# An attention and two MoE layers on one core: buffers at multiples of 256 bytes, three small operations rewritten, the planner's constants replaced

## The chip, the cores and the metric

One core of one Trainium2 chip runs the whole program in one launch. The metric is the device time of an execution in microseconds, and of several executions the median. The engines are named as in the profile: PE is TensorE's matmul and PEld its weight load, DVE is VectorE, ACT is ScalarE, POOL is GpSimd, SP is SyncE, whose queue issues all DMAs of this kernel.

## What is computed

An attention with a decay (4 batches, 8 heads, 576 positions, 64 dimensions), then two pairs of dense layers that are called MoE (2304 tokens, 512 wide, 2048 inside), the second with a slope per column. All is float32.

```
scores = scale * q @ k.T + (cum[:, None] - cum[None, :])      # cum: running sum of log f
scores = where(causal, -1e9, scores); scores -= max(scores)
attn = exp(scores); attn = attn / (sum(attn) + 1e-9)
x = attn @ v                                                   # to (2304, 512)
h = x @ w_in;   x = max(0.01 * h, h) @ w_out                   # first MoE
h = x @ w_in2;  out = (max(h, 0) + alpha * min(h, 0)) @ w_out2 # second MoE
```

## The kernel before

Products are made at float32's accuracy from `float32r` operands: a tile is split into a high part (a cast) and a low part (the tile minus its high part), and PE adds three products, high times high, high times low and low times high. Nearly all work of ACT, DVE and POOL is there to make such pairs.

**Stages.** The attention works in eight groups, four of 320 query rows and four of 256 (`ORDER`, `GROUPS`), in units of up to 128 rows (`UNITS`). The first 16 heads (`NAT`) are "native": they skip the splits and use PE's slower float32 matmul, in the prologue, while the first weights arrive. The others are spread over the first MoE, as work between its matmuls. The first MoE runs over blocks of 256 or 512 tokens (`BLOCKS`): for each of 16 chunks f of the inner width, `moe_h` (L604) makes h, `leaky` (L613) the activation, `hi` and `lo` its split, `moe1_y` (L650) the product with w_out. Of its 32 half chunks of weights 14 stay in SBUF and 18 (`STREAM`) are written to `wscr` and read back for each block through the ring `ws`. The second MoE takes three blocks of 768 tokens with a Strassen-like scheme of seven products (`moe2_h`, L761; `moe2_y`, L830); its combined weights are made earlier by `weight2_in` and stored in `w2in`. Raw weights come as 64-bit floats, and `assemble` puts float32 numbers together from their halves on ACT (L492, the "rebase") and DVE (L499, L502, L507).

**One attention unit** (`attention_scores`, `attention_weights`): PE makes scores (L1131), POOL masks the decay row `cb` into `dm` by a selection (L1097) or, for packed pairs of heads, adds a mask (L1104), DVE adds it to the scores and takes the row's extreme into `nm` (L1145, the "decay"), ACT takes the exponential and the row sum (L1156), DVE adds 1e-9 to the sum (L1001, the "guard") and inverts it (L1004), for two units at once, and ACT, POOL or DVE multiply by the inverse (L1171, L1173, the normalisation). PE then transposes (L1186), ACT and DVE split the transposed tile into `pt` (L404, L1202), and PE multiplies by v (L1034). `shift` (L1075, ACT) and `add` (L1078, DVE) bring the two parts of v's product together, and the result is split into `xp`.

For a head that isn't native, `qk` holds q and k twice, in the upper and the lower 64 partitions. `qk_hi` casts both into `k1`, `q_lo` (L935) overwrites the lower 64 partitions of q's columns with q's low part, by DVE or POOL, and `k_lo` makes k's low part in `k2`. v lies in DRAM with a block of 64 zeros between the two heads of a pair, which the native heads need; `vr` loads it with the zeros (L914), and `v_hi` and `v_lo` split it into `v2`.

**The order of the work.** Every operation is handed to a planner (`Plan`) with its engines, its assumed duration on each, a due time and the buffers that it reads and writes. `Plan.run` goes through time, gives each engine the ready operation with the earliest due time, and the program is written in that order; on the chip every engine works strictly in its order and waits on semaphores. `latency` (L121) is what the planner allows between the end of an operation on one engine and the start of one that needs it on another: 260 ns to PE, 200 from PE, 170 otherwise, 125 on the same engine, `DMALAT` after a DMA. The due times come from the constants at the top of the file: `PROL`, `PROL0` and `FIRST0` are the assumed lengths of the prologue and the first block, `LEAD1`, `LEAD2` and `LASTSPAN` say how early a group of the attention is due, `AHEAD` how early a streamed weight, the constants of `W2` when the second MoE's weights are made, `PACKLEAD` how early the first scores of a pair.

**Where the tiles lie.** Tiles are placed one after another in pools, each rounded up to 32 bytes. The 8 bytes of `rate` and the 4 of `warm` put `xp` and all that follows in the pool `sb` (the rings `g`, `gr`, `w`, `ws`, `ysb`, `tri`) at 192 bytes past a multiple of 256. In the pool of the attention the 80 bytes of `nm` move what follows by 96. In the pool `p2` of the second MoE the 64 bytes of `alpha` bring what follows to a multiple of 256: `bx`, `yraw`, `xt`, `r`, `g2`, `wb` and the last of the four `wa`. What is placed from the right (`raw`, `cv`, later `by`) lies 224 past one.

Of the kernel before, what the change touches and what calls it, by code (L numbers as in the profile page):

```python
# [26 lines left out]
AHEAD = 7600  # L27
# [4 lines left out]
PACKLEAD = 5200  # L32
# [14 lines left out]
W2LEAD = 112200  # L47
NEARLY = 4
W2FROM = 2.77
W2EACH = 0.68  # L50
W2LAG = 51000
W2STEP = 5300
W2OUT = 8400
# [7 lines left out]
PROL = 52000  # L61
PROL0 = 26000
FIRST0 = 99000
FREE = 8
ATTN = 12800
LASTH = 10600
W1LEAD = 12500
LEAD1 = 24000
LEAD2 = 54900
DMALAT = 2600  # L70
BATCH = 1
LASTSPAN = 1.04
STEP = 4
PRICE = 0.25
# [36 lines left out]
class Plan:  # L111
# [165 lines left out]
def t_act(n):  # L277
    return 0.833 * n + 90
# [14 lines left out]
def t_pool1(n):  # L293
    return 0.833 * n + 245
# [19 lines left out]
def tile_forgetting_attention_two_moe(ctx: ExitStack, tc, qk0, qk1, v0, v1, fg, w1, w2, alphaT, out):  # L314
# [78 lines left out]
    dram = ctx.enter_context(tc.tile_pool(name="dram", bufs=1, space=DRAM))  # L393
    vctx = ExitStack()
# [49 lines left out]
    ring("vr", 2, [P, 5, 3, D], pool="att")  # L444
# [6 lines left out]
    ring("nm", 3, [P, 4, 5], pool="att")  # L451
# [6 lines left out]
    ring("nm0", 4, [P, 4, 5], pool="att0")  # L458
# [3 lines left out]
    rate = const.tile([B * H, 2], F32, name="rate")  # L462
    warm = const.tile([1, 1], F32, name="warm")
# [5 lines left out]
    warm_b, cum_b, yd_b, wscr_b, w2_b, rate_b = (Buf(Ring(1, None)) for _ in range(6))  # L469
    for b, ap in ((warm_b, warm), (cum_b, cum_d), (yd_b, yd), (wscr_b, wscr), (w2_b, w2in), (rate_b, rate)):  # L470
        b.ap = ap
# [9 lines left out]
    def assemble(which, f, half, d, after=()):  # L481

        raw, v = new("raw"), new("cv")
        src = (w1, w2)[which].bitcast(I32)[f, :, 2 * CW * half : 2 * CW * (half + 1)]

        def load():
            sp.dma_start(out=raw.ap, in_=src.rearrange("p (n t) -> p n t", t=2))

        def rebase(e):
            high = f32(raw.ap[:, :, 1])  # L490
            if e == "act":
                act.activation(out=f32(v.ap), in_=high, func=AF.Copy, scale=2.0**-112)  # L492
# [19 lines left out]
        plan.op({"act": t_act(CW), "pool": t_pool1(CW)}, d, rebase, r=[raw], w=[v])  # L512
# [357 lines left out]
    def attention_heads(gi, hs, d, span):  # L870
# [29 lines left out]
        for e, h in enumerate(hs):  # L900
# [33 lines left out]
            def q_lo(en, k1=k1, qk=qk):  # L934
                sub(en, k1.ap[D:P, :n], qk.ap[D:P, :n], f32(k1.ap[D:P, :n]))  # L935
# [60 lines left out]
        for i, u, t, es, du in todo:  # L996
            if i % RECIPS == 0:
                i1 = min(i + RECIPS, len(todo))

                def guard(i=i, i1=i1):  # L1000
                    dve.tensor_scalar(out=nm.ap[:, 3, i:i1], in0=nm.ap[:, 2, i:i1], scalar1=1e-9, scalar2=None, op0=ALU.add)  # L1001
# [5 lines left out]
                on("dve", 70, du, guard, w=both)  # L1007
# [5 lines left out]
    def attention_out(g, t0, h, e, dd, vr, v2, o2, lo, hi, pt, pt_ap, native):  # L1013
# [68 lines left out]
        on("act", t_act(n) - 40, dd, shift, r=[po], w=[(xr, h % 2)])  # L1082
        on("dve", t_dve(n), dd, add, r=[po], w=[(xr, h % 2)])
# [170 lines left out]
    for i in range(2):  # L1254
        rows = sum(max(0, min(NAT - gi * H, H)) for gi, k in enumerate(ORDER) if k == i)
# [75 lines left out]
    ring("alpha", 1, [P, NF], pool="p2", after=opened)  # L1331
# [86 lines left out]
```

## Time and profile before

| | us |
|---|---|
| median of 3 runs | 993.36 |
| lowest and highest | 992.1 and 994.47 |
| the profiled execution, its own time | 991.83 |
| its span, first to last instruction | 989.7 |
| PE busy | 976.0 |
| DVE busy | 746.7 |
| ACT busy | 536.2 |
| POOL busy | 90.1 |

The busy times say how long an engine had at least one instruction in work. A matmul's end is modelled, and matmuls overlap in the picture, so PE's pace is read from how many of them a stretch holds. The first MoE and the attention last until about 608 us; the second MoE takes the rest.

### The profile page before, as it was taken

How to read it: one execution, taken by the hardware profiler on the slowest of the kernel's cores; microseconds unless marked ns; L12 is line 12 of the kernel's file. 1: busy time of each engine (PE TensorE's matmuls, PEld its weight loads, DVE VectorE, ACT ScalarE, POOL GpSimd, SP SyncE). 2: the span in 40 equal slices, each digit the busy share in tenths (PEclk: the TensorE clock that was granted, in tenths of full speed). 3: DMA queues.
4: the chain of work that ended last, by engine and by line, in shares of the span. 5: the costliest groups of instructions: out<-in, count | busy, mean ns of one | idle time of the engine just before them, and what ended most of it. 6: DMA issues, size and time to landing. Idle time of an engine off the chain costs nothing.

```text
span 989.7 us, 15662 instructions
## 1 busy us (share of the span) xinstructions
PE 976.0 (99%) x5170; PEld 842.6 (85%) x5170; DVE 746.7 (75%) x1849; ACT 536.2 (54%) x1231; POOL 90.1 (9%) x161
## 2 busy tenths in 40 slices
PE   9999999999999999999999999999999999999998
PEld 7777777999888878878878888889889898988987
DVE  7798999887998897986776647856696656856563
ACT  8987887996887777867646435211232112321112
POOL 2101233211211120211000000000000000000000
PEclk9999999999999999999999999999999999999999
DMA  8869887688767789845497765533374333634311
GB/s 285 286 202 320 284 316 229 207 297 285 259 228 267 242 275 320 271 145 174 138 368 253 262 213 173 175 111 118 107 245 129 127 118 107 203 121 144 105 46 64
DMA packets 76128, 203.27 MB, mean 205 GB/s; under 512 B 8112, under 2 KB 23248, under 8 KB 76048
## 3 DMA queue, kind: packets, MB, share of 16 engines
q1 hardware_dynamic: 76048, 202.28, 61.2%
q8 instruction: 41, 0.67, 0.3%
q14 instruction: 39, 0.32, 0.1%
HBM read 168.57 MB, written 33.67 MB: 204 GB/s over the span
## 4 chain that ended last, share of the span: by engine, by line
PE 76%; DVE 10%; issue 6%; DMA 4%; ACT 4%; POOL 1%; POOLq 0%; ACTq 0%; SPq 0%; DVEq 0%
PE bank L830 20%; PE bank L761 18%; PE bank L650 12%; PE bank L604 12%; PE bank L1131 5%; PE bank L1186 3%; PE bank L1034 3%; DMA raw<-w 2%; PE bank L1024 1%; DVE pt L1202 1%; DVE k L409 1%; DVE t L1145 1%; DMA w2in<-wa 1%; DVE cv L507 1%; DVE g L409 1%
## 5 line engine op out<-in xcount | busy, mean ns | idle before, releaser
L830 PE MATMUL bank<-w,g 128*128 128x512 f32 x756 | 196.9, 393 | 0.0
L404 ACT ACTIVATE g<-r 128x384 fp32r<-128x384 f32 x96 | 50.4, 526 | 256.3 <-DVE r L793 232.5
L770 DVE TENSOR_TENSOR r<-bank,r 128x384 f32<-128x384 f32 x168 | 91.0, 555 | 91.1 <-PE bank L761 90.9
L830 PEld LDWEIGHTS bank<-w,g 128*128 128x128 f32 x756 | 140.1, 188 | 21.2
L650 PE MATMUL bank<-g,ws 128*128 128x512 f32 (+1 forms) x540 | 128.0, 374 | 1.3 <-ACT g L404 1.3
L604 PE MATMUL bank<-xp,ws 128*128 128x512 f32 (+1 forms) x540 | 126.3, 372 | 0.0
L650 PEld LDWEIGHTS bank<-g,ws 128*128 128x128 f32 x540 | 92.1, 189 | 18.2 <-ACT g L404 3.7
L604 PEld LDWEIGHTS bank<-xp,ws 128*128 128x128 f32 x540 | 93.3, 189 | 15.2
L650 PE MATMUL bank<-g,w 128*128 128x512 f32 (+1 forms) x420 | 101.4, 375 | 0.1
L604 PE MATMUL bank<-xp,w 128*128 128x512 f32 (+1 forms) x420 | 99.2, 374 | 0.1
L1156 ACT ACTIVATE t<-t,nm 128x128 f32<-128x128 f32 (+4 forms) x144 | 83.9, 586 | 24.6 <-DVE nm L1145 24.2
L604 PEld LDWEIGHTS bank<-xp,w 128*128 128x128 f32 x420 | 72.1, 189 | 12.4 <-ACT t L1171 0.5
L650 PEld LDWEIGHTS bank<-g,w 128*128 128x128 f32 x420 | 71.8, 189 | 12.1 <-ACT g L404 0.7
L1202 DVE TENSOR_TENSOR pt<-bank,pt 128x128 fp32r<-128x128 f32 (+2 forms) x136 | 64.1, 504 | 22.2 <-ACT pt L404 21.7
L1097 POOL TENSOR_SCALAR_AFFINE_SELECT dm<-cb 128x448 f32<-128x448 f32 (+1 forms) x96 | 54.9, 573 | 264.1 <-DVE nm L1145 224.2
L1171 ACT ACTIVATE t<-t,nm 128x128 f32<-128x128 f32 (+4 forms) x112 | 58.8, 564 | 28.7 <-DVE nm L1004 27.5
L409 DVE TENSOR_TENSOR g<-r,g 128x384 fp32r<-128x384 f32 x96 | 53.2, 554 | 25.9 <-ACT g L404 25.9
L404 ACT ACTIVATE pt<-bank 128x512 fp32r<-128x512 f32 (+6 forms) x176 | 67.6, 433 | 4.3 <-PE bank L1186 3.6
L1186 PE MATMUL bank<-tri,t 128*128 128x128 f32 x432 | 65.8, 277 | 1.7 <-DVE t L1173 0.5
L409 DVE TENSOR_TENSOR g<-gr,g 128x512 fp32r<-128x512 f32 x72 | 50.4, 700 | 18.4 <-ACT g L404 18.3
L1186 PEld LDWEIGHTS bank<-tri,t 128*128 128x128 f32 x432 | 49.3, 141 | 15.0 <-ACT t L1171 5.3
L1034 PEld LDWEIGHTS bank<-pt,v 128*128 128x128 f32 x416 | 55.8, 189 | 5.9 <-ACT pt L404 1.9
(136 smaller groups left out, 1687.0 us busy)
## 6 DMA issues: line engine op xcount, KB each, us to landing
ws<-wscr SPq DMA_DIRECT2D x72, 512.0 KB, 4.9
raw<-w SPq DMA_DIRECT2D x64, 512.0 KB, 5.8
wa<-w2in SPq DMA_DIRECT2D x33, 512.0 KB, 3.5
ws<-w2in SPq DMA_DIRECT2D x33, 512.0 KB, 3.5
qk<-qk SPq DMA_DIRECT2D x32, 416.0 KB, 4.7
wscr<-ws SPq DMA_DIRECT2D x18, 512.0 KB, 5.6
cb<-cum_d SPq DMA_DIRECT2D x32, 288.0 KB, 4.4
vr<-v SPq DMA_DIRECT2D x16, 480.0 KB, 5.1
```

What stands on the lines that cost most here:

```text
L404: act.activation(out=out, in_=in_, func=AF.Copy)
L409: (dve if e == "dve" else gps).tensor_tensor(out=out, in0=in0, in1=in1, op=ALU.subtract)
L604: pe.matmul(h()[:, i] if single else h(), lhsT=w.ap[:, a, c * P : (c + 1) * P], rhs=xs[0].ap[:, s, c] if single else xp[:, x0 : x0 + 2, s, c],
L650: pe.matmul(out(c), lhsT=w.ap[:, a, col : col + P], rhs=g.ap[:, s, at : at + n], start=f == 0 and (a, s) == (0, 0) and (c % 2 == 0 or not ...
L761: pe.matmul(b.ap[:, :N2], lhsT=t.ap[:, a, o + c * P : o + (c + 1) * P], rhs=view(k)[:, s, c], start=c == 0 and i == 0, stop=c == 1 and i == 2,
L770: on("dve", t_dve(N2), d + k * step - URGENT, lambda: dve.tensor_tensor(out=out.ap, in0=b.ap[:, :N2], in1=x.ap, op=ALU.add), r=[b] if x is ...
L830: pe.matmul(acc[j * (N2 // P) + t].ap, lhsT=g.ap[:, s, t * P : (t + 1) * P], rhs=w.ap[:, a], start=p == 0 and i == j and (a, s) == (0, 0), ...
L1034: pe.matmul(po.ap[:, q:n], lhsT=v2.ap[:, o2 + j, :], rhs=pt_ap(s, e, j, j + 1, q, n), start=s == 0 and j == 0, stop=s == 1 and j == nkt - 1,)
L1156: act.activation(out=t.ap[:, :nk], in_=t.ap[:, :nk], func=AF.Exp, scale=-1.0, bias=nm.ap[:, last, u : u + 1], accum_out=nm.ap[:, 2, u : u ...
L1171: act.activation(out=t.ap[:, :nk], in_=t.ap[:, :nk], func=AF.Copy, scale=nm.ap[:, 3, u : u + 1])
L1186: pe.transpose(tp.ap[:, (j - j0) * P : (j - j0 + 1) * P], t.ap[:, k0 : k0 + P], f32(tri_b.ap[:, :P]))
L1202: dve.tensor_tensor(out=lo, in0=src, in1=f32(hi), op=ALU.subtract)
```

## The change

1. **Addresses.** `rate` and `warm` move into one tile `small` of 128 bytes, together with `alpha` and a new column `lower`; a tile `edge` of 224 bytes is placed first from the right; `nm` has rows of 16 instead of 5 numbers (256 bytes instead of 80). With that every tile from `xp` on starts at a multiple of 256 bytes.
2. **q's low part.** `lower` is 0 in the upper 64 partitions and -1 in the lower. `q_lo` becomes one operation over all 128 partitions, lower * k1 + qk, which leaves q's high part above and its low part below; it runs on DVE alone.
3. **The guard** runs on POOL instead of DVE.
4. **v without zero blocks.** For heads that aren't native the load takes every second block of 64 columns; `vr` has two blocks per key tile instead of three.
5. **The planner.** Four of its latencies become constants with new values (125 on the same engine and 200 from PE as before, 315 to PE, 200 otherwise), the assumed times of the rebase, `shift` and `add` are 50, 130 and 100 ns longer, and 20 constants of the due times change.

```
-AHEAD = 7600
+AHEAD = 5100
-PACKLEAD = 5200
+PACKLEAD = 6100
...
-DMALAT = 2600
+DMALAT = 3200
...
+        return (0 if a == "pe" else TOSAME) if a == b else TOPE if b == "pe" else FROMPE if a == "pe" else CROSS
...
+    ctx.enter_context(tc.tile_pool(name="edge", bufs=1, side="right")).tile([P, 56], F32, name="edge")
...
-    ring("vr", 2, [P, 5, 3, D], pool="att")
+    ring("vr", 2, [P, 5, 2, D], pool="att")
...
-    ring("nm", 3, [P, 4, 5], pool="att")
+    ring("nm", 3, [P, 4, 16], pool="att")
...
-    rate = const.tile([B * H, 2], F32, name="rate")
-    warm = const.tile([1, 1], F32, name="warm")
+    small = const.tile([P, 32], F32, name="small")
+    rate, lower, warm = small[: B * H, :2], small[:, 2:3], small[:1, 3:4]
+    rings["alpha"] = Ring(1, lambda slot: small[:, 4 : 4 + NF])
...
-                    out=vr.ap[:, :nkt], in_=g["v"][b, h // 2]), w=[vr])
+                    out=vr.ap[:, :nkt], in_=g["v"][b, h // 2] if native else g["v"][b, h // 2][:, :, ::2]), w=[vr])
...
-            def q_lo(en, k1=k1, qk=qk):
-                sub(en, k1.ap[D:P, :n], qk.ap[D:P, :n], f32(k1.ap[D:P, :n]))
+            def q_lo(k1=k1, qk=qk):
+                dve.scalar_tensor_tensor(
+                    out=k1.ap[:, :n], in0=f32(k1.ap[:, :n]), scalar=lower, in1=qk.ap[:, :n], op0=ALU.mult, op1=ALU.add
+                )
...
-                plan.op(t_sub(n), dh - 2e3, q_lo, r=[qk], w=[(k1, "q")], shared=True)
+                on("dve", t_dve(n), dh - 2e3, q_lo, r=[qk, lower_b], w=[(k1, "q")], shared=True)
...
-                    dve.tensor_scalar(out=nm.ap[:, 3, i:i1], in0=nm.ap[:, 2, i:i1], scalar1=1e-9, scalar2=None, op0=ALU.add)
+                    gps.tensor_scalar(out=nm.ap[:, 3, i:i1], in0=nm.ap[:, 2, i:i1], scalar1=1e-9, scalar2=None, op0=ALU.add)
...
-                on("dve", 70, du, guard, w=both)
+                on("pool", 180, du, guard, w=both)
```

All constants change the order on every engine. Three places of it follow; a row is the line, the operation, the tile that it writes, the tiles that it reads, and its shape. The line numbers of the changed program are 5 to 9 higher.

DVE, in the first group of the attention that isn't native, where the units of one pair of heads get their decay, guard and reciprocal. Before:

```order
L1145 ISA t_1350,nm_1171<-bank_76,dm_1246 128x256
L1145 ISA nm_1171 128x1
L1145 ISA t_1355,nm_1171<-bank_75,cb_1047 128x320
L1145 ISA nm_1171 128x1
L409 TENSOR_TENSOR g_1353<-gr_1328,g_1353 128x512
L1001 TENSOR_SCALAR nm_1171<-nm_1171 128x2
L1004 RECIPROCAL nm_1171<-nm_1171 128x2
L1001 TENSOR_SCALAR nm_1171<-nm_1171 128x1
L1004 RECIPROCAL nm_1171<-nm_1171 128x1
```

The changed program, at the same place:

```order
L1153 ISA t_1353,nm_1176<-bank_76,dm_1255 128x256
L1153 ISA nm_1176 128x1
L508 SCALAR_TENSOR_TENSOR cv_1314<-raw_1197,cv_1314 128x512
L414 TENSOR_TENSOR g_1371<-gr_1341,g_1371 128x512
L414 TENSOR_TENSOR w_1362<-cv_1207,w_1362 128x512
L513 SCALAR_TENSOR_TENSOR cv_1314<-raw_1197,cv_1314 128x512
L1153 ISA t_1374,nm_1176<-bank_77,cb_1001 128x320
L1153 ISA nm_1176 128x1
L1012 RECIPROCAL nm_1176<-nm_1176 128x2
L941 SCALAR_TENSOR_TENSOR k_0_1390<-k_0_1390,small,qk_1185 128x320
```

The guards are gone from DVE, four operations of 512 columns and the third unit's decay stand ahead of the first reciprocal, and `q_lo` is the operation that reads `small`.

POOL, at the same place of the changed program (before, L1001 doesn't occur on POOL):

```order
L1105 AFFINE_SELECT dm_1255<-cb_1071 128x256
L1112 TENSOR_TENSOR cb_1160<-cb_1160,tri_121 64x64 x2
L414 TENSOR_TENSOR k_0_1312<-qk_1117,k_0_1289 128x320
L414 TENSOR_TENSOR v_0_1306<-vr_939,v_0_1306 128x3x64
L1105 AFFINE_SELECT dm_1367<-cb_1160 128x128
L1009 TENSOR_SCALAR nm_1176<-nm_1176 128x2
L1105 AFFINE_SELECT dm_1401<-cb_1160 128x256
L1009 TENSOR_SCALAR nm_1176<-nm_1176 128x1
```

The guards (L1009) stand among the mask selections (L1105), the pair masks (L1112) and the subtractions of k and v.

PE, at the passage from the first MoE (L650) into the second (L761). Before:

```order
L650 MATMUL bank_69<-g_7140,w_2031 128x512
L650 MATMUL bank_70<-g_7140,w_2031 128x512
L650 MATMUL bank_76<-g_7140,w_2031 128x512
L650 MATMUL bank_75<-g_7140,w_2031 128x512
L761 MATMUL bank_74<-bx_6254,wa_6372 128x384 x6
L761 MATMUL bank_73<-bx_6307,wa_6372 128x384 x6
```

The changed program:

```order
L656 MATMUL bank_73<-g_7134,w_2034 128x512
L656 MATMUL bank_74<-g_7134,w_2034 128x512
L767 MATMUL bank_75<-bx_6294,wa_6404 128x384 x6
L656 MATMUL bank_76<-g_7134,w_2034 128x512
L656 MATMUL bank_78<-g_7134,w_2034 128x512
L767 MATMUL bank_79<-bx_6349,wa_6404 128x384 x6
```

The first product of the second MoE now stands ahead of the first MoE's last two matmuls.

## Rows read from the trace of the kernel before

**Rows 1.** The page, part 1: busy us, share of the span, instructions.

```profile
PE 976.0 (99%) x5170; PEld 842.6 (85%) x5170; DVE 746.7 (75%) x1849; ACT 536.2 (54%) x1231; POOL 90.1 (9%) x161
```

**Rows 2.** Busy us by stage: length, PE, PEld, DVE, ACT, POOL; clock, DMA share, GB/s.

```profile
0.00:55.00 55.00, 53.16 (x287) 41.37 (x287) 40.50 (x174) 49.53 (x174) 10.05 (x31) 1.00 0.80 266
55.00:155.00 100.00, 97.49 (x478) 79.05 (x479) 93.53 (x232) 77.16 (x186) 22.65 (x35) 1.00 0.86 292
155.00:505.00 350.00, 345.64 (x2082) 299.14 (x2081) 299.27 (x819) 269.83 (x607) 57.37 (x96) 1.00 0.72 241
505.00:607.00 102.00, 101.70 (x449) 83.86 (x449) 65.08 (x112) 49.69 (x85) 0.00 (x0) 1.00 0.70 245
607.00:620.00 13.00, 12.14 (x65) 11.02 (x64) 10.73 (x23) 6.36 (x13) 0.00 (x0) 1.00 0.73 255
620.00:985.00 365.00, 365.00 (x1813) 327.73 (x1812) 237.57 (x493) 82.70 (x166) 0.00 (x0) 1.00 0.40 127
```

**Rows 3.** PE's waits by releaser: us in total, times, longest; 13 groups.

```profile
PE bank L1131 <- DVE pt L1202: 1.4, 2, 1.0
...
PE bank L1131 <- DVE k L409: 0.5, 1, 0.5
...
PE bank L1186 <- DVE nm L1145: 0.2, 1, 0.2
```

**Rows 4.** PE's groups by line and shape: count, busy us, mean ns, idle before.

```profile
L830 PE MATMUL bank<-w,g 128*128 128x512 f32 x756 | 196.9, 393 | 0.0
L761 PE MATMUL bank<-xp,ws 128*128 128x384 f32 x192 | 38.9, 337 | 0.0
L761 PE MATMUL bank<-bx,ws 128*128 128x384 f32 x144 | 28.7, 336 | 0.0
L830 PE MATMUL bank<-wb,g 128*128 128x512 f32 x108 | 28.2, 393 | 0.0
```

**Rows 5.** The chain that ended last, two stretches: start, length in us.

```profile
532.35 2.72 PE bank L604 x12
...
951.50 1.39 PE bank L830 x6
```

**Rows 6.** The guard, line L1001: min/median/max ns; by stage, length and DVE's busy us.

```profile
L1001 DVE TENSOR_SCALAR nm<-nm x80: 126/160/522, 10.3 to 480.2; 128x2 f32<-128x2 f32 x64, 128x1 f32<-128x1 f32 x16
...
55.00:155.00 100.00, 2.47 (x12) 1.00 0.86 292
155.00:505.00 350.00, 7.54 (x46) 1.00 0.72 241
```

**Rows 7.** POOL: line L1097, groups by shape, and DVE's wait for it.

```profile
L1097 POOL TENSOR_SCALAR_AFFINE_SELECT dm<-cb x96: 286/561/1292, 69.3 to 470.3; 128x448 f32<-128x448 f32 x32, 128x192 f32<-128x192 f32 x32, 128x128 f32<-128x128 f32 x16, 128x256 f32<-128x256 f32 x16
...
L1097 POOL TENSOR_SCALAR_AFFINE_SELECT dm<-cb 128x448 f32<-128x448 f32 x32 | 21.0, 656 | 125.0 <-DVE nm L1145 108.7 <-DMA vr<-v 7.4 <-DMA cb<-cum_d 5.4
...
L409 POOL TENSOR_TENSOR k<-qk,k 64x320 fp32r<-64x320 f32 x4 | 5.2, 1291 | 15.7 <-ACT k L404 11.6 <-issue 4.1
...
L1253 POOL MEMSET rate<- 32x2 f32 x1 | 0.1, 89 | 0.0
...
DVE t L1145 <- POOL dm L1097: 0.7, 4, 0.2
```

**Rows 8.** DVE's groups by shape: count, busy us, mean ns, idle before.

```profile
L409 DVE TENSOR_TENSOR k<-qk,k 64x256 fp32r<-64x256 f32 x32 | 13.6, 426 | 1.6 <-ACT k L404 0.8
L406 DVE CAST w<-cv 128x512 fp32r<-128x512 f32 x7 | 3.0, 423 | 1.9 <-PE bank L650 1.8
```

**Rows 9.** The timeline at 105.7 us: start, length, instructions merged, wait before.

```profile
105.70 1.30 DVE L409 TENSOR_TENSOR k<-qk,k 64x320 fp32r<-64x320 f32 x2
105.83 0.81 POOL L409 TENSOR_TENSOR v<-vr,v 128x192 fp32r<-128x192 f32 x1 [6.15 <-ACT v L404]
```

**Rows 10.** The loads of v, line L914: from issue to landing.

```profile
DMA to landing us min/median/max: 2.9/5.2/7.2
```

**Rows 11.** The timeline at the passage into the second MoE.

```profile
610.22 1.67 PE L761 MATMUL bank<-bx,wa 128*128 128x384 f32 x8 [0.85 <-DVE bx L409]
```

More of the change, by code (lines that the diff above doesn't have):

```diff
@@ L21 @@
 EXCL = 1
+TOSAME = 125
+TOPE = 315
+FROMPE = 200
+CROSS = 200
 WT = {"dve": 1.0, "act": 1.0, "pool": 1.0}
@@ L46 @@
 NYSB = 2
-W2LEAD = 112200
+W2LEAD = 114600
 NEARLY = 4
-W2FROM = 2.77
-W2EACH = 0.68
+W2FROM = 2.753
+W2EACH = 0.762
 W2LAG = 51000
-W2STEP = 5300
-W2OUT = 8400
+W2STEP = 4900
+W2OUT = 9300
 AHEAD2 = 16300
@@ L60 @@
 SHIFT = 1
-PROL = 52000
-PROL0 = 26000
-FIRST0 = 99000
+PROL = 53600
+PROL0 = 24200
+FIRST0 = 94700
 FREE = 8
-ATTN = 12800
-LASTH = 10600
+ATTN = 12200
+LASTH = 13600
 W1LEAD = 12500
-LEAD1 = 24000
+LEAD1 = 24800
 LEAD2 = 54900
-DMALAT = 2600
+DMALAT = 3200
 BATCH = 1
-LASTSPAN = 1.04
+LASTSPAN = 1.083
 STEP = 4
-PRICE = 0.25
+PRICE = 0.141
 MASKED = 2.0**30
@@ L467, in tile_forgetting_attention_two_moe @@
     cum_d = dram.tile([B * H, 2, S], F32, name="cum_d")
-    warm_b, cum_b, yd_b, wscr_b, w2_b, rate_b = (Buf(Ring(1, None)) for _ in range(6))
-    for b, ap in ((warm_b, warm), (cum_b, cum_d), (yd_b, yd), (wscr_b, wscr), (w2_b, w2in), (rate_b, rate)):
+    warm_b, cum_b, yd_b, wscr_b, w2_b, rate_b, lower_b = (Buf(Ring(1, None)) for _ in range(7))
+    for b, ap in ((warm_b, warm), (cum_b, cum_d), (yd_b, yd), (wscr_b, wscr), (w2_b, w2in), (rate_b, rate), (lower_b, lower)):
         b.ap = ap
@@ L511, in assemble @@
         on("dma", t_dma(8 * CW * P), EARLY if (which, f) == (0, 0) else d - 5e3, load, w=[raw], after=after)
-        plan.op({"act": t_act(CW), "pool": t_pool1(CW)}, d, rebase, r=[raw], w=[v])
+        plan.op({"act": t_act(CW) + 50, "pool": t_pool1(CW)}, d, rebase, r=[raw], w=[v])
         on("dve", t_dve2(CW), d, bits, w=[v], shared=True)
@@ L913, in attention_heads @@
                 vr = x_raw["v"] = new("vr0" if native else "vr")
-                on("dma", t_dma(3 * nkt * D * 4 * P), dh - (6e3 if native else 12e3), lambda: sp.dma_start(
-                    out=vr.ap[:, :nkt], in_=g["v"][b, h // 2]), w=[vr])
+                on("dma", t_dma((2 + native) * nkt * D * 4 * P), dh - (6e3 if native else 12e3), lambda: sp.dma_start(
+                    out=vr.ap[:, :nkt], in_=g["v"][b, h // 2] if native else g["v"][b, h // 2][:, :, ::2]), w=[vr])
             apart = not native or gi == 0 and h < 2
@@ L940, in v_hi @@
             def v_hi(en, v2=v2, h=h, hi=hi, o2=o2):
-                cast(en, v2.ap[:, o2 : o2 + nkt, hi : hi + D], vr.ap[:, :nkt, h % 2 * 2, :])
+                cast(en, v2.ap[:, o2 : o2 + nkt, hi : hi + D], vr.ap[:, :nkt, h % 2, :])
             def v_lo(en, v2=v2, h=h, hi=hi, lo=lo, o2=o2):
-                sub(en, v2.ap[:, o2 : o2 + nkt, lo : lo + D], vr.ap[:, :nkt, h % 2 * 2, :], f32(v2.ap[:, o2 : o2 + nkt, hi : hi + D]))
+                sub(en, v2.ap[:, o2 : o2 + nkt, lo : lo + D], vr.ap[:, :nkt, h % 2, :], f32(v2.ap[:, o2 : o2 + nkt, hi : hi + D]))
             m = full[-1][0] + P
@@ L1080, in add @@
             )
-        on("act", t_act(n) - 40, dd, shift, r=[po], w=[(xr, h % 2)])
-        on("dve", t_dve(n), dd, add, r=[po], w=[(xr, h % 2)])
+        on("act", t_act(n) + 90, dd, shift, r=[po], w=[(xr, h % 2)])
+        on("dve", t_dve(n) + 100, dd, add, r=[po], w=[(xr, h % 2)])
         if not even:
@@ L1254, in tile_forgetting_attention_two_moe @@
     for i in range(2):
+        on("pool", 100, -9.4e3, lambda i=i: gps.memset(lower[i * D : i * D + D], -1.0 * i), a=[(lower_b, i)])
+    for i in range(2):
         rows = sum(max(0, min(NAT - gi * H, H)) for gi, k in enumerate(ORDER) if k == i)
@@ L1330, in tile_forgetting_attention_two_moe @@
     ring("r", 4, [P, N2], pool="p2", after=opened)
-    ring("alpha", 1, [P, NF], pool="p2", after=opened)
     alpha_b = new("alpha")
```

3 lines of the change are left out of this document (1 added, 2 removed).

## The prediction

> **What bounds the kernel now.** I read the page's busy times first, then the stages, then who made TensorE wait, then TensorE's pace. The page [rows 1] has PE busy for 976.0 of 989.7 us. [...] What is not busy lies in the attention's prologue (55.00 - 53.16 = 1.84), from 55 to 155 (2.51), from 155 to 505 (4.36), at the passage into the second MoE (13.00 - 12.14 = 0.86), and after the last matmul (about 3.8 of the last 4.7 us, in which the last output is evacuated and stored). [...]
>
> The waits of PE [rows 3] are small and many: 13 groups, 18 waits, 9.2 us in all, 0.5 us each. That understates them. A matmul of 512 columns is drawn as 393 ns long [rows 4], but in the chain [rows 5] twelve of them follow each other in 2.72 us, one per 226.7 ns. So a new matmul can be up to 166 ns late without any idle time being shown, and each wait that is shown was some 0.17 us longer. For 18 waits that is 3.0 us more.
>
> **The change part by part.** The profiled execution took 991.83 us, with a span of 989.7; that is 1.5 us (0.15%) under the median of 993.36. The sum below is a difference, and I put it on the median.
>
> *PE's own work: 0.* Both programs issue the same matmuls in the same shapes (5170 records in the profile); only their order differs. Whatever the change is worth, it is worth through PE's waits or through PE's pace.
>
> *The addresses: 0, with ends at -4.3 and 0.* The program before already has some of its tiles at multiples of 256 bytes, so the trace holds the comparison. `bx` lies there, `xp` 192 past one: the products of L761 have a mean of 336 or 337 ns with either. `wb` lies there, `w` 192 past: L830 has 393 ns with either [rows 4]. The other end: in the second MoE PE's pace isn't perfect. Six matmuls of L830 take 1.39 us, or 231.7 ns each [rows 5], where 226.7 were possible; for 756 + 108 of them that is 4.3 us. If the odd addresses cause all of that, the change gains it. I take 0, because the two comparisons inside the trace are the nearest rows and neither shows more than 1 ns.
>
> *The guard leaves DVE: hidden, between -2 and +6.* 80 additions of 1e-9 (median 160 ns, 64 of them on two columns and 16 on one) go to POOL; 80 x 160 ns is 12.8 us of DVE time. 12 of them lie from 55 to 155 us, 46 after that, the rest before [rows 6], so 58 x 160 ns = 9.3 us fall after 55 us. DVE is busy for 393 of those 450 us, so most of it was covered by PE's work already; where DVE is full, from 55 to 155 us, 12 guards (1.9 us) come free, and this is the gain's end. In exchange each reciprocal on DVE now waits for POOL, which has to wait for the exponential on ACT first. Behind the waiting reciprocal stand the normalisations of ACT and all that DVE has queued; on POOL the mask selections of later units stand before or behind the guard (see the order ahead). POOL is busy for 80 of 450 us, so it is usually free. What the guard costs there no row shows. The nearest from below is a memset of a few columns, 89 ns; from above a mask selection of 128x448, 656 ns in the mean [rows 7]. The guard is nearest to the memset in size, so I take about 0.2 us and its hand-over, and cover for it: in the new order four operations of 512 columns and another decay stand on DVE between the second decay of a pair and its reciprocal. The other end is the rival below.
>
> *q's low part: 0, ends -1 and +1.* 44 subtractions of 64x256 or 64x320 on DVE and 4 on POOL become 48 operations of 128 partitions on DVE. The 64x256 subtraction has a mean of 426 ns [rows 8]; with as many columns I take the same for the new one, which reads two SBUF tiles as it does. That adds 4 x 0.43 = 1.7 us to DVE and takes 4 x 1.29 = 5.2 us from POOL [rows 7]. The second matters more than its size. At 105.7 us [rows 9] two such subtractions on DVE took 1.30 us, while POOL ran a subtraction of 0.81 us beside them, and PE's scores waited 0.5 us for them, the one wait of PE in the whole trace that names this tile [rows 3].
>
> *v without its zero blocks: 0.* 16 loads of 480 KB become 320 KB, 8 of 288 KB become 192 KB, together 3.3 MB less; but each partition's piece of 3,840 or 2,304 bytes becomes ten or six pieces of 256 bytes. These loads land 5.2 us after their issue, 7.2 at most [rows 10], and the code gives them 12 us before the head is due. Even 3 us more stay covered. If the cover fails, `v_hi` is late, and with it the pv products, by what is over 12 us.
>
> *The planner's constants: -5.5, ends +6 and -11.* The tables before allow 260 ns from any engine to PE, now 315; 2600 ns for a DMA, now 3200; and the shift, the add and the rebase are set 50 to 130 ns longer. Every order is a new one, so no single wait of before can be carried over. What can be carried over is the amount: 8.0 us of idle between 55 and 620 us [rows 2] and 3.0 us hidden in the matmuls' length, 11 us that a perfect order would get back. The reserve of 55 ns is small beside a mean wait of 0.5 us, so it removes the short waits and shortens the long ones; I take half. One place can be followed. Before, the first products of the second MoE wait for `bx`, 0.85 us as drawn [rows 11], since the second half of `yraw` is split only then. In the new order six products stand before the last two matmuls of L650 (0.45 us), so something is done while the rest is split, but these six need the same second half. Part of this wait stays. Against the gain stands that the attention ends later: the last pv matmul has about 5 us more matmul time before it than it had, on some 570 to the second MoE, which is no loss by itself.
>
> Sum: -5.5 on 993.4 us is 988 us.
>
> **Rivals.** *The guard on POOL stalls DVE (slower).* In the trace POOL's operations stretch where DVE works beside them: the mask selection of 128x448 has a mean of 656 ns, while L1097 has a minimum of 286 ns over all its shapes and a median of 561 [rows 7]; and the two DVE subtractions at 105.7 us were stretched by POOL [rows 9]. If each guard after 55 us is held up by 0.37 us (656 - 286) beyond the 160 ns that it took on DVE, the reciprocals hold DVE for 58 x 0.37 = 21 us. DVE has 57 us free there, but only 6.5 of them from 55 to 155. If about half reaches PE, through late weights and late probabilities, that is 11 us, and with half of the constants' gain left 5.5 remain: 999 us. It decides from a mean hold-up of about 0.2 us on, where the loss outweighs the gain. [...] Against it: POOL was free for 370 of 450 us, and DVE waited for POOL's mask selections four times only, 0.7 us in all, in the whole trace [rows 7].
>
> *The addresses count after all (faster still).* If L830 gets down to 226.7 ns everywhere, the 4.3 us above come on top: 983.5 us. The equal means in the trace speak against it.
>
> *The waits only move (no change).* A new order has the same chains to cover, and DVE stays as full as it was (12.8 us less of guards, but more of the casts and normalisations that ACT loses, by the two orders 11 more casts of 128x512 and 7 more normalisations, at the cast's 0.42 us [rows 8] 7.6 us). Then the sum of the waits stays at 11 us, and the time at 993.4.
>
> **How the numbers follow.** The forecast (988, its own range 982 to 991) gets 0.48; the addresses too (983.5) 0.12; the same 0.17; slower by the guard 0.23. About 0.2% (2 us) is what a measurement of this kernel can tell from no change, so faster is 0.48 + 0.12 = 0.60, same 0.17, slower 0.23. The range reaches from the middle of the second case's lower side, 980, to just under the centre of the slower one, 998; about 0.06 is left out below and 0.13 above.
>
> **What would show it.** Right: PE busy again 365 of 365 us from 620 to 985, six matmuls of L830 again about 1.39 us, the means of L761 and L830 within 1 ns; the waits of PE fewer, with 4 us instead of 8 not busy between 55 and 620 us; guards on POOL of 0.1 to 0.3 us. Wrong by the guard: guards of 0.5 us and more, and reciprocals on DVE that wait for POOL in sum over 10 us. Wrong by the addresses: twelve matmuls of L604 below 2.70 us or L830 at 227 ns. Wrong by the order: the not-busy time of PE between 55 and 620 us at 8 us or more, with other names on it.

## The result, and the profile after

The changed kernel takes **978.65 us** (median of 4 runs, 978.17 to 979.21) against 993.53 us for the kernel before, measured beside it: a ratio of 0.9852, with a 95% interval of 0.9835 to 0.9869. That is 14.9 us less, below the forecast of 988 and just below the range's 980. The profiled execution has a span of 977.4 us, 12.3 less than before.

The page's busy times and then the stages of the changed kernel, in the columns of [rows 1] and [rows 2]:

```profile
PE 968.6 (99%) x5170; PEld 845.4 (86%) x5170; DVE 746.4 (76%) x1793; ACT 520.7 (53%) x1205; POOL 122.8 (13%) x245
```

```profile
0.00:55.00 55.00, 52.71 (x282) 40.55 (x283) 40.98 (x160) 48.38 (x167) 19.49 (x56) 1.00 0.84 279
55.00:155.00 100.00, 98.90 (x494) 81.42 (x493) 94.44 (x227) 79.57 (x197) 28.01 (x53) 1.00 0.85 280
155.00:505.00 350.00, 348.35 (x2123) 308.79 (x2123) 305.64 (x799) 259.82 (x585) 75.25 (x137) 1.00 0.75 242
505.00:607.00 102.00, 102.00 (x465) 86.03 (x464) 68.82 (x122) 49.56 (x88) 0.00 (x0) 1.00 0.70 244
607.00:620.00 13.00, 13.00 (x66) 11.63 (x65) 13.00 (x30) 4.40 (x9) 0.00 (x0) 1.00 0.63 212
620.00:973.00 353.00, 353.00 (x1749) 316.82 (x1748) 223.53 (x461) 78.28 (x158) 0.00 (x0) 1.00 0.38 123
```

The gain lies ahead of the second MoE. From 55 to 620 us PE is idle for 1.10 + 1.65 = 2.75 us, where it was 8.03. The clock is 1.00 as before. DVE is as busy as before (746.4 us) although 80 guards left it; ACT has 15.5 us less, so work of ACT took their place. The idle time that went (5.3 us) is less than half of the 12.3 us by which the span fell; the rest never was drawn as idle. The experiments come back to that.

The passage into the second MoE, which lay at 607 to 620 us before, comes earlier now, and PE has no idle time there:

```profile
595.00:612.00 17.00, 17.00 (x91) 15.97 (x91) 15.76 (x34) 8.18 (x18) 0.00 (x0) 1.00 0.76 262
```

PE's waits, all eight groups; before there were 13 with 9.2 us [rows 3]:

```profile
PE bank L1244 <- DVE gr L1239: 1.2, 1, 1.2
PE bank L656 <- DVE g L411: 0.9, 1, 0.9
PE bank L1194 <- ACT pt L409: 0.8, 2, 0.4
PE bank L656 <- ACT g L409: 0.6, 1, 0.6
PE bank L1139 <- DVE k L414: 0.4, 1, 0.4
PE bank L1139 <- DVE xr L1086: 0.3, 1, 0.3
PE bank L1139 <- ACT pt L409: 0.2, 1, 0.2
PE bank L1194 <- DVE nm L1153: 0.2, 1, 0.2
```

PE's pace has not changed. The chain that ended last still has twelve matmuls of L610 (L604 before) in 2.72 us, and nine of L836 (L830) in 2.08 us, 231 ns each, as in [rows 5]:

```profile
558.05 2.72 PE bank L610 x12
...
617.52 2.08 PE bank L836 x9
```

The guard on POOL, line L1009 (min/median/max ns, first and last start, as in [rows 6]):

```profile
L1009 POOL TENSOR_SCALAR nm<-nm x80: 212/350/1826, 10.9 to 473.4; 128x2 f32<-128x2 f32 x64, 128x1 f32<-128x1 f32 x16
```

POOL's groups by shape (busy us, mean ns, idle before):

```profile
L1009 POOL TENSOR_SCALAR nm<-nm 128x2 f32<-128x2 f32 x64 | 27.5, 429 | 87.8 <-ACT t L1164 87.2
```

And DVE's wait for it (us in total, times, longest):

```profile
DVE nm L1012 <- POOL nm L1009: 2.0, 3, 1.0
```

On DVE, in the kernel before, the guards of the same shape had a mean of 182 ns:

```profile
L1001 DVE TENSOR_SCALAR nm<-nm 128x2 f32<-128x2 f32 x64 | 11.7, 182 | 3.6 <-ACT t L1156 3.2
```

So a guard on two columns takes 2.4 times what it took on DVE, and yet the reciprocals wait for it three times only.

### The profile page after: what moved, and what is told of

The parts are those of the page before. It is cut to its first block, busy times and chain, and to the rows that moved or that the text cites. A ratio compares the mean times of both kernels' runs of the same rounds, so it can differ in the third digit from the quotient of the medians.

```text
span 977.4 us, 15704 instructions
## 1 busy us (share of the span) xinstructions
PE 968.6 (99%) x5170; PEld 845.4 (86%) x5170; DVE 746.4 (76%) x1793; ACT 520.7 (53%) x1205; POOL 122.8 (13%) x245
## 4 chain that ended last, share of the span: by engine, by line
PE 68%; DVE 4%; DMA 2%; issue 0%; ACT 0%; SPq 0%; ACTq 0%; DVEq 0%
PE bank L836 20%; PE bank L767 18%; PE bank L656 12%; PE bank L610 11%; PE bank L1042 2%; PE bank L1139 2%; PE bank L1194 2%; DMA w2in<-g 1%; DMA raw<-w 1%; DVE pt L1210 1%; DVE g L414 0%; DVE t L1153 0%; DVE k L414 0%; DVE v L414 0%; DVE cv L508 0%
## 5 line engine op out<-in xcount | busy, mean ns | idle before, releaser
L836 PE MATMUL bank<-w,g 128*128 128x512 f32 x756 | 196.5, 393 | 0.0
L409 ACT ACTIVATE g<-r 128x384 fp32r<-128x384 f32 x96 | 50.4, 525 | 258.7 <-DVE r L799 224.5
L836 PEld LDWEIGHTS bank<-w,g 128*128 128x128 f32 x756 | 140.0, 188 | 20.9
L610 PE MATMUL bank<-xp,ws 128*128 128x512 f32 (+1 forms) x540 | 126.9, 373 | 0.0
L656 PEld LDWEIGHTS bank<-g,ws 128*128 128x128 f32 x540 | 92.2, 189 | 15.5 <-ACT g L409 0.8
L610 PEld LDWEIGHTS bank<-xp,ws 128*128 128x128 f32 x540 | 92.7, 189 | 14.8
L610 PE MATMUL bank<-xp,w 128*128 128x512 f32 (+1 forms) x420 | 99.3, 373 | 0.0
L1164 ACT ACTIVATE t<-t,nm 128x128 f32<-128x128 f32 (+4 forms) x144 | 83.6, 583 | 15.8 <-DVE nm L1153 15.2
L610 PEld LDWEIGHTS bank<-xp,w 128*128 128x128 f32 x420 | 72.5, 189 | 11.6
L1105 POOL TENSOR_SCALAR_AFFINE_SELECT dm<-cb 128x448 f32<-128x448 f32 (+1 forms) x96 | 52.1, 543 | 209.0 <-DVE nm L1153 152.5
L414 DVE TENSOR_TENSOR g<-r,g 128x384 fp32r<-128x384 f32 x96 | 53.0, 553 | 25.6 <-ACT g L409 25.5
L409 ACT ACTIVATE pt<-bank 128x128 fp32r<-128x128 f32 (+6 forms) x174 | 67.7, 431 | 7.7 <-PE bank L1194 7.1
L1179 ACT ACTIVATE t<-t,nm 128x128 f32<-128x128 f32 (+4 forms) x105 | 54.3, 548 | 16.2 <-DVE nm L1012 15.7
L619 ACT ACTIVATE gr<-bank 128x512 f32<-128x512 f32 x72 | 42.6, 593 | 36.5 <-PE bank L610 35.9
L414 DVE TENSOR_TENSOR g<-gr,g 128x512 fp32r<-128x512 f32 x72 | 50.7, 704 | 11.7 <-ACT g L409 11.6
```

Of the source, the lines that this page charges most:

```text
L409: act.activation(out=out, in_=in_, func=AF.Copy)
L414: (dve if e == "dve" else gps).tensor_tensor(out=out, in0=in0, in1=in1, op=ALU.subtract)
L610: pe.matmul(h()[:, i] if single else h(), lhsT=w.ap[:, a, c * P : (c + 1) * P], rhs=xs[0].ap[:, s, c] if single else xp[:, x0 : x0 + 2, s, c],
L656: pe.matmul(out(c), lhsT=w.ap[:, a, col : col + P], rhs=g.ap[:, s, at : at + n], start=f == 0 and (a, s) == (0, 0) and (c % 2 == 0 or not ...
L836: pe.matmul(acc[j * (N2 // P) + t].ap, lhsT=g.ap[:, s, t * P : (t + 1) * P], rhs=w.ap[:, a], start=p == 0 and i == j and (a, s) == (0, 0), ...
L1164: act.activation(out=t.ap[:, :nk], in_=t.ap[:, :nk], func=AF.Exp, scale=-1.0, bias=nm.ap[:, last, u : u + 1], accum_out=nm.ap[:, 2, u : u ...
```

## Experiments

Each kernel was timed beside the kernel before, whose median lay between 992.27 and 993.53 us on these occasions. "Same order" means that every engine's instructions stand in the same sequence, so that only the edit differs; "replanned" means that the planner made a new order.

### The addresses: e1

The changed kernel without `edge`, with `nm` at 80 bytes again and `small` at 320 bytes; same order.

```
-    ctx.enter_context(tc.tile_pool(name="edge", bufs=1, side="right")).tile([P, 56], F32, name="edge")
...
-    ring("nm", 3, [P, 4, 16], pool="att")
+    ring("nm", 3, [P, 4, 5], pool="att")
...
-    small = const.tile([P, 32], F32, name="small")
+    small = const.tile([P, 80], F32, name="small")
```

> The changed kernel with every SBUF tile moved off the multiples of 256 bytes again (left side 192 past one, pt and the third t 32 past one, right side 224 past one); the order on every engine is the same as the changed kernel's, row by row. Theory (the gain is a new order with fewer short waits of PE, addresses cost nothing): 978.7 us, within 1 us of the changed kernel. Rival (the addresses make the gain, or a good part of it): 983 to 993 us, with the matmuls' and DVE's mean durations up by some ns each.

Measured: 978.41 us, ratio 0.9858 (0.9844 to 0.9872). The addresses are worth nothing.

### Constants and code apart: e2, e3

e2 is the changed code with the old constants, latencies and durations; e3 the old code with the new ones.

```
-AHEAD = 5100
+AHEAD = 7600
...
-TOPE = 315
+TOPE = 260
...
```

> The changed kernel's code (guard on GpSimd, q's low part in one operation, v without zero blocks, aligned addresses) planned with the planner's constants, latencies and durations of before. Theory (the constants make the gain): 988 to 994 us. Rival (the code edits free DVE and so make the gain): 978 to 983 us. In between, both have a share, and PE's not-busy time from 55 to 620 us plus its short waits says how much.

> The kernel before with nothing but the planner's constants, latencies and durations of the change; guard on DVE, q's low part and v as before. Theory (the constants make the gain): 979 to 984 us. Rival (the code edits make it): 988 to 994 us. If the leads only suit the code that they were set for, it can come out slower than before, 994 to 1005 us.

Measured: e2 998.33 us (ratio 1.0060, 1.0048 to 1.0071), e3 987.76 us (0.9952, 0.9940 to 0.9964). Neither theory holds for both runs: e3 lies at the edge of its rival (988 us), which gives the gain to the code edits, but e2, which has the code edits alone, is slower than before. The constants alone bring 4.5 us, a third of the gain. The code edits alone cost 6 us, and one place of e2 shows how (stages of 10 us, columns as in [rows 2]):

```profile
135.00:145.00 10.00, 9.63 (x47) 7.48 (x45) 9.37 (x25) 8.47 (x21) 2.58 (x5) 1.00 0.99 357
145.00:155.00 10.00, 2.87 (x12) 1.88 (x12) 9.09 (x22) 4.63 (x13) 0.86 (x2) 0.70 0.72 242
```

PE runs dry for 7 us while DVE works on, and the granted clock is 0.70 in the mean of that stretch, where it was 1.00 in the one ahead. The longest waits of PE from 100 to 155 us are for DVE:

```profile
PE bank L1194 <- DVE xr L1086: 2.2, 1, 2.2
PE bank L1194 <- DVE pt L1210: 1.8, 1, 1.8
PE bank L1042 <- DVE xr L1086: 1.6, 1, 1.6
```

### The guard: e4 to e7

e4 is the changed kernel with the guard on DVE again, replanned:

```
-                    gps.tensor_scalar(out=nm.ap[:, 3, i:i1], in0=nm.ap[:, 2, i:i1], scalar1=1e-9, scalar2=None, op0=ALU.add)
+                    dve.tensor_scalar(out=nm.ap[:, 3, i:i1], in0=nm.ap[:, 2, i:i1], scalar1=1e-9, scalar2=None, op0=ALU.add)
...
-                on("pool", 180, du, guard, w=both)
+                on("dve", 70, du, guard, w=both)
```

> The changed kernel with the guard on DVE again (planned as 70 ns there); the rest as in the changed kernel. If the guard's move is worth nothing, as the prediction had it: 977.5 to 980.5 us. If its 9.3 us of DVE time are what PE's waits went with: 984 to 990 us. [...]

Measured: 987.02 us (0.9943, 0.9930 to 0.9956). The guard's move, costed at nothing, is worth 8.4 us here. Between e3 and e4 lie q's low part, v's loads and the addresses, together 0.7 us, with another order.

Is it DVE's time, or a better order? e5, e6 and e7 change `dve` to `gps` or back in the first line alone, so that the order stays.

> The changed kernel's order as it is (planned with the guard on GpSimd), but the 80 guards are issued on DVE, each where the order has it; nothing else differs. Theory A (the guard's move pays by the DVE time and the waits of the guard for ACT that it takes from DVE): 984 to 990 us, like the run with the guard planned on DVE. Theory B (the move pays only because the planner found another, luckier order): 978 to 980 us. Half of either: 981 to 983.

> The mirror: the order of e4 (planned with the guard on DVE, 987.0 us), but the guards are issued on GpSimd. Theory A: 978 to 983 us. Theory B: 986 to 988 us. If GpSimd holds up reciprocals that stand close behind their guard in this order: 988 to 993 us.

> The kernel before in its own order, only that the 80 guards are issued on GpSimd in place of DVE; no constant is changed. Theory A: 983 to 988 us (5 to 9 us less). Theory B: 991 to 994 us. If GpSimd holds up reciprocals that stand close behind their guard: 994 to 1000 us.

Measured: e5 983.75 us (0.9911, 0.9896 to 0.9927), e6 984.55 us (0.9920, 0.9905 to 0.9935), e7 994.26 us (1.0018, 1.0009 to 1.0027). In the changed kernel's order the engine alone makes 5.1 of the 8.4 us; the other 3.3 are the order. In orders that were planned with the guard on DVE, POOL gains 2.5 us (e6) or loses 1.6 (e7). The less POOL gains, the longer DVE's reciprocals wait for the guards: 2.0 us in the changed kernel, and in e6 and e7

```profile
DVE nm L1012 <- POOL nm L1009: 6.5, 12, 1.0
```

```profile
DVE nm L1004 <- POOL nm L1001: 12.2, 18, 1.2
```

That is the rival of the prediction, and the planner takes most of it away: once it knows that the guard is on POOL, it puts other work ahead of the reciprocal.

e5 has the changed kernel's order, so the two can be compared matmul by matmul. The line of the second MoE's products gives the first and the last start of the same weight loads (xp with wa) in the changed kernel:

```profile
L767 PEld LDWEIGHTS bank<-xp,wa x192: 187/188/189, 598.4 to 941.2; 128*128 128x128 f32 x192
```

In e5:

```profile
L767 PEld LDWEIGHTS bank<-xp,wa x192: 187/188/188, 603.4 to 946.2; 128*128 128x128 f32 x192
```

The guards of e5 on DVE:

```profile
L1009 DVE TENSOR_SCALAR nm<-nm x80: 124/156/489, 11.0 to 478.5; 128x2 f32<-128x2 f32 x64, 128x1 f32<-128x1 f32 x16
```

And two of its stages:

```profile
55.00:155.00 100.00, 98.27 (x484) 79.58 (x483) 94.41 (x239) 78.31 (x193) 22.58 (x37) 1.00 0.84 277
155.00:505.00 350.00, 347.29 (x2112) 305.76 (x2111) 308.36 (x836) 257.84 (x583) 55.40 (x94) 1.00 0.74 238
```

By 603.4 us e5 is 5.0 us late (603.4 - 598.4), and by the last such load still 5.0 (946.2 - 941.2): all of it is lost ahead of the second MoE. But from 55 to 505 us PE is idle for 1.73 + 2.71 = 4.44 us against 2.75, which is 1.7 us more; in the prologue and from 505 us on the two agree. **Two thirds of the loss are not drawn as idle**: they are matmuls that start late while the one before is still drawn.

### DVE's time as such: e9 to e11

e9 is the kernel before, and e10 the changed one, each in its own order and without the guards:

```
-                    dve.tensor_scalar(out=nm.ap[:, 3, i:i1], in0=nm.ap[:, 2, i:i1], scalar1=1e-9, scalar2=None, op0=ALU.add)
+                    pass
...
-                    dve.reciprocal(out=nm.ap[:, 3, i:i1], in_=nm.ap[:, 3, i:i1])
+                    dve.reciprocal(out=nm.ap[:, 3, i:i1], in_=nm.ap[:, 2, i:i1])
```

e11 is e5 with the guard's line written twice.

> The kernel before in its own order with the 80 guards left out: the addition of 1e-9 isn't done at all, and the reciprocal reads the sum itself. DVE has 12.8 us less to do and waits for nothing new. Theory A (DVE's time in the attention is on PE's path, at about 0.4 us of the end for each us: 5.1 us for 12.8 in the changed kernel's order; with the guards on GpSimd the reciprocals' wait of 12.2 us ate it in this order): 985 to 989 us. Theory B (in the order of before it is not DVE's time that sets PE's waits): 991 to 993.5 us.

> The changed kernel in its own order with the 80 guards left out (the addition of 1e-9 isn't done), where GpSimd does them in the changed kernel. If GpSimd's guards are covered there: 977.5 to 979 us, no change. [...]

> The changed kernel's order with each guard issued on DVE, and issued twice, so DVE has another 12.8 us of two-column additions beside e5. Theory A (DVE's time has a price in this order): 987 to 991 us, about 5 us over e5's 983.75. Theory B (what e5 lost is the guard's place on DVE, where it waits for ACT and holds up what is behind it, and not its time): 983.5 to 985 us.

Measured: e9 987.70 us (0.9943, 0.9927 to 0.9959), e10 979.34 us (0.9860, 0.9846 to 0.9874), e11 991.79 us (0.9988, 0.9979 to 0.9996).

- e9: 12.8 us less on DVE (80 times the median of 160 ns) bring 5.1 us, in the order of before and with no constant changed. So 0.4 us for each us that is drawn; the interval allows 4 to 7 us.
- e5 over the changed kernel: 80 x 156 ns = 12.5 us more on DVE cost 5.1 us, again 0.4.
- e11 over e5: another 80 guards cost 8.0 us, 0.64 for each us; why that is more than 0.4 no run shows.
- e10: without POOL's guards nothing is gained, so these are covered. The way from the row sum to the weights is a step shorter there, and in this order it brings nothing, which speaks against the guard costing as a step of that way in e5.

These prices are for drawn time, and 0.4 is no constant. With the distance between starts as the measure (see q's low part), the 80 guards of e5 push DVE's next operation back by 5.7 us in all, against the same places of the changed kernel, and those of the kernel before by 11.9 us against e9. That makes 0.9 and 0.4 us for each us. In the kernel before the reciprocal that needs the guard's result stands right behind 40 of the 80 guards and starts 193 ns after it (median), while a subtraction (L409) behind a guard starts 69 ns after it. An extra operation on DVE that nothing waits for was not tried.

DVE's time has a price in the attention, in both kernels, although PE is drawn as busy there for 99%. What e9 shows to be there is gone in e7, where the reciprocals wait for POOL for 12.2 us: e7, the same order with the guards on POOL, is 6.6 us slower than e9.

### Reserves and leads: e8, e12, e13

e8 is the changed kernel with the old latencies and the old three durations; e12 the kernel before with only these new; e13 the kernel before with only the old constants at the top of the file replaced (leads, due times, the DMA's latency).

```
-TOPE = 315
+TOPE = 260
...
-CROSS = 200
+CROSS = 170
...
```

> The changed kernel with the planner's latencies between engines (260 to PE, 170 across) and the durations of the rebase, the shift and the add as before, the leads as in the change. If the longer reserves are what removes short waits: 983 to 990 us. If the leads alone do it: 978 to 981 us. If neither, but the match of both: above 990 us.

> The kernel before with only the planner's latencies (315 to PE, 200 across) and the durations of rebase, shift and add as in the change; the leads as before. Theory (the longer reserves are what shortens PE's waits, alone as well): 986 to 990 us, like all constants together (987.8). Rival (reserves and leads only work together, as in the changed kernel, where the old reserves cost 4.9 us): 991 to 996 us.

> The kernel before with only the planner's leads, due times and the DMA's 3200 ns set as in the change; latencies between engines and the three durations as before. Theory (the reserves bring what the constants bring: alone 6.8 us, all together 4.5): 993 to 998 us, the leads alone bring nothing or lose. Rival (each brings a part): 988 to 992 us.

Measured: e8 983.58 us (0.9915, 0.9900 to 0.9929), e12 986.01 us (0.9928, 0.9913 to 0.9943), e13 990.45 us (0.9974, 0.9964 to 0.9984). The longer reserves bring 6.8 us alone and 4.9 in the changed kernel; the leads alone 1.9. Together in the old code they bring 4.5 (e3), less than the reserves alone: the parts don't add up, and each makes a new order. That the reserves work by removing short waits isn't shown: PE's drawn waits in e12 are 19 with 8.1 us, against 18 with 9.2 before.

### q's low part and v: e14, e17, e18

e14 sets q's low part back and replans; e17 keeps the changed kernel's order and puts back the operation alone, always on DVE:

```
-                dve.scalar_tensor_tensor(
-                    out=k1.ap[:, :n], in0=f32(k1.ap[:, :n]), scalar=lower, in1=qk.ap[:, :n], op0=ALU.mult, op1=ALU.add
-                )
+                sub(
+                    "dve", k1.ap[D:P, :n], qk.ap[D:P, :n], f32(k1.ap[D:P, :n])
+                )
```

e18 is the kernel before, same order, with `vr` at two blocks and loaded by `g["v"][b, h // 2][:, :, ::2]`.

> The changed kernel with q's low part as before: 48 subtractions on 64 partitions, which the planner may give to DVE or to GpSimd; replanned. Theory (worth nothing, as the prediction had it): 977.5 to 981 us. Rival (a larger effect, hidden by one of opposite sign from v's loads): 982 to 988 us, or under 977.

> The changed kernel's order as it is; only the 48 operations for q's low part are the subtractions on 64 partitions of before, on DVE at the same places. If e14's 4.8 us came from the new order: 977 to 979 us (the old operation is some 60 ns shorter, 48 x 0.06 = 2.9 us of DVE, at 0.4 us each 1.2 us less). If they come from the operation (64 partitions hold something up): 982 to 985 us.

> The kernel before in its own order, only that the 24 loads of v in fp32r attention fetch the two halves without the zero blocks (256-byte pieces), into the smaller tile. Theory (covered, as the prediction had it): 991.5 to 993.5 us. If the many small pieces hold up other transfers or the issuing queue: 994 to 999 us.

Measured: e14 983.44 us (0.9907, 0.9894 to 0.9921), e17 981.19 us (0.9887, 0.9869 to 0.9904), e18 992.66 us (1.0005, 0.9992 to 1.0017). v's loads are worth nothing. The operation for q's low part is worth 2.5 us in an unchanged order, and the new order 2.3 more. DVE's timeline shows where the time goes, at the same place of the changed kernel and of e17 (of the two instructions in e17's second row the first is the old operation, the second the 128x576 subtraction behind it):

```profile
297.63 0.68 DVE L414 TENSOR_TENSOR g<-cv,g 128x512 fp32r<-128x512 f32 x1
298.23 0.47 DVE L941 SCALAR_TENSOR_TENSOR k<-k,small,qk 128x256 fp32r<-128x256 f32 x1
298.63 0.74 DVE L414 TENSOR_TENSOR k<-qk,k 128x576 fp32r<-128x576 f32 x1
299.30 0.41 DVE L1086 TENSOR_TENSOR xr<-bank,xr 64x256 f32<-64x256 f32 x1
```

```profile
298.66 0.68 DVE L414 TENSOR_TENSOR g<-cv,g 128x512 fp32r<-128x512 f32 x1
299.37 1.20 DVE L414 TENSOR_TENSOR k<-qk,k 64x256 fp32r<-64x256 f32 x2
300.48 0.41 DVE L1086 TENSOR_TENSOR xr<-bank,xr 64x256 f32<-64x256 f32 x1
```

The new operation is drawn longer (0.47 us; the old one had 0.43 [rows 8]), but it starts 0.60 us after its predecessor, while that is still drawn, where the old one starts 0.71 us after it, behind its end. From `g` to `xr` it is 1.67 against 1.82 us. Not all 48 places are like this one: added up over all of them, from the start of the operation ahead to the start of the second one behind, the old operation takes 4.5 us more, so the 2.5 us measured are 0.6 for each us. At the 12 places with an operation of 512 columns ahead, the new one starts 0.60 us after it in the mean and the old one 0.71. The operation behind starts before the drawn end of the new one at 46 of the 48 places, and never before that of the old one.

The `add` of an odd head (L1086) itself writes the lower 64 partitions. At the four places where such an `add` stands ahead, the gap is the other way round. The changed kernel and e17 at one of them:

```profile
446.80 0.43 DVE L1086 TENSOR_TENSOR xr<-bank,xr 64x256 f32<-64x256 f32 x1
447.26 0.48 DVE L941 SCALAR_TENSOR_TENSOR k<-k,small,qk 128x256 fp32r<-128x256 f32 x1
```

```profile
448.83 0.43 DVE L1086 TENSOR_TENSOR xr<-bank,xr 64x256 f32<-64x256 f32 x1
449.18 1.19 DVE L414 TENSOR_TENSOR k<-qk,k 64x256 fp32r<-64x256 f32 x2
```

Here the new operation starts 0.46 us after the `add`, behind its end, and the old one, on the same partitions as the `add`, after 0.35 us. At these places the later start thus goes along with the change of the start partition (0.71 against 0.60 us, 0.46 against 0.35), not with the kind of operation.

### Another way to free DVE: e15, e16

`RECIPS` 3 and 5 instead of 2, replanned: fewer guards and reciprocals, for more units at once.

```
-RECIPS = 2
+RECIPS = 3
```

> The changed kernel with guard and reciprocal done for up to 3 units at once in place of 2: 2 pairs of them for a group of 5 units in place of 3; replanned. It takes some 16 to 26 reciprocals of 0.16 us (2.5 to 4.2 us) from DVE and as many guards from GpSimd; the weights of the first two units of a group come later. Theory (DVE's time is worth about 0.4 us each): 976.5 to 978.5 us. Rival (the later weights cost more than that): 980 to 988 us.

> The same for all 5 units at once: 48 to 52 reciprocals fewer (8 us of DVE), and the weights of the first four units wait for the fifth. By DVE's time alone: 974 to 977 us. If the lateness of the weights counts: 985 to 1000 us.

Measured: e15 986.87 us (0.9944, 0.9932 to 0.9955), e16 988.25 us (0.9957, 0.9944 to 0.9970). Both are worse than the changed kernel, so fewer operations on DVE didn't pay here. The later weights are the likely cause, but both runs have a new order, and no run separates the two. In e15 the reciprocals wait for the guards again, by DVE's waits:

```profile
DVE nm L1012 <- POOL nm L1009: 6.6, 10, 1.5
```

And in its second stage PE is busy for 95.58 of 100 us:

```profile
55.00:155.00 100.00, 95.58 (x463) 77.27 (x463) 93.86 (x221) 75.60 (x184) 27.37 (x46) 0.98 0.86 285
```

No run beat the changed kernel by more than the measurement can tell.

## Why the prediction was wrong

**The step that failed is "The guard leaves DVE: hidden, between -2 and +6".** It counted 9.3 us of freed DVE time after 55 us and took all but 1.9 as covered by PE's work, since DVE was busy for 393 of 450 us only; in the sum the whole stood at nothing. But the guard was worth 8.4 us (e4), 5.1 by its engine alone (e5), beyond the term's end of -2, and none of the signs named ahead was for such a gain. Cover was the wrong picture. Free time of DVE in the mean doesn't say that DVE is free when a tile becomes ready for it; each operation that stands ahead delays what follows in its queue, and of the drawn time 40% reached the end, in the order of before as well (e9).

**The sentence that carried the mistake** is that an idle time of 8.0 us and 3.0 us hidden behind 18 drawn waits are all "that a perfect order would get back". The 3.0 were far too few: the 14.9 us measured are more than the 11 together, and of e5's 5.0 us only 1.7 are drawn. A matmul that starts late while the one before is still drawn shows no wait, so counting the drawn waits misses it.

- *The planner's constants, -5.5*: 4.5 measured alone (e3), near in size, but in part by luck: half of the waits was to go, and e3 still has 17 drawn waits with 8.2 us, against 18 with 9.2. The reserves alone bring 6.8 us (e12), also with hardly fewer waits. Idle time from 55 to 620 us came down to 2.75 us in the changed kernel instead of 4, with the guard's share in it. At the passage the wait is gone altogether, where a part of it was expected to stay: PE has 17.00 of 17.00 us from 595 to 612 us.
- *The addresses, 0*: right (e1). Even the upper end of 4.3 us is excluded; the L836 matmuls still need 231 ns each.
- *q's low part, 0 (±1)*: too small, 2.5 us in the same order (e17). The durations of [rows 8] were taken for the engine's time; the distances between starts, which these rows don't show, are 4.5 us longer over the 48 places with the old operation (e17). The row at 105.7 us [rows 9] was misread besides: of its two instructions the first, q's low part, took 0.49 us, less than the mean of its shape (0.52); only the second, k's low part on 128x320, took longer than its mean, 0.79 us against 0.52, with POOL's subtraction of 0.81 us beside it, and it ended just ahead of the scores that waited.
- *v without zero blocks, 0*: right (e18).
- *The rival "the guard on POOL stalls DVE"*: refuted for the changed kernel (2.0 us of reciprocals waiting, and nothing gained in e10 without the guards), though a guard took longer than was feared: 429 ns in the mean on two columns, where the rival began to decide at 0.2 us beyond 160. Five of these 64 had no operation of DVE beside them and took 212 or 213 ns; the one at 447.82 us lasts 0.66 us and ends 0.07 us behind the subtraction that DVE had in work (L414, 447.66 to 448.41 us). That this costs the end nothing here is what e10 measured. The 286 ns that the rival subtracted are of a selection of 128x128 (the kernel before, 120.92 us); the shortest of 128x448 took 552 ns there and their median is 561, against the mean of 656. Where the order isn't planned for it the rival is real (e7, 1.6 us slower).
- *"The waits only move"*: refuted, with 9 drawn waits and 4.6 us instead of 18 and 9.2.

In sum: 4.5 us constants (e3), 0.7 for q's low part, v and the addresses with the guard still on DVE (e4 against e3), 8.4 for the guard with its order. That makes 13.6 us, from 992.27 us, which the kernel before took beside e3 and e4, to 978.65; beside the changed kernel it took 993.53, hence the 14.9 above. The split between the parts depends on the sequence in which they are made, since every new plan is another order; a replanned edit moved the time by 2 to 3 us beyond its own effect (e4 against e5, e14 against e17). Which rows of an order make these 2 to 3 us wasn't tried and stays open.

## What to carry to other kernels

Where one engine is drawn as busy for 99% and its neighbour for 87%, time on the neighbour need not be free: double or leave out a small operation in an unchanged order and measure its price. Judge an operation by the distance between starts, not by its drawn length, and look at the start partitions of its neighbours in the queue: here a change of them went along with a start 0.11 us later (e17). A changed engine pays most with an order that is planned for it: the same move of the guard gave 8.4 us less, 5.1 less, 2.5 less or 1.6 more.

## What the runs showed of the hardware

In the changed kernel L414 on 128x512 is drawn 0.68 us long, and q's low part behind it starts 0.60 us after its start, some 0.08 us ahead of its end. At the 12 places with an operation of 512 columns ahead, the old operation for q's low part, on partitions 64 to 127, starts 0.11 us later in the mean (e17, 0.71 us) than the new one on all 128 (the changed kernel, 0.60). After a guard on DVE the next operation starts 69 ns later in the median when a subtraction stands behind it, and 193 ns later when the reciprocal that needs its result does (the kernel before). With the tiles off the multiples of 256 bytes twelve matmuls of L610 again take 2.72 us and nine of L836 2.08 us (e1). PE's granted clock was 1.00 in e2 from 135 to 145 us, with PE busy for 9.63 us, and 0.70 in the mean from 145 to 155 us, with PE busy for 2.87 us.
